# Linear attention and a gated feed-forward on one core: a new order of the steps, with trios of tiles, quartered w1 and closed first gate units

## The chip, the cores and the metric

The kernel runs on one core of a Trainium2 chip. A core has five engines that run side by side and meet through semaphores: TensorE (PE for its products and transposes, PEld for its weight loads), VectorE (DVE), ScalarE (ACT), GpSimd (POOL) and SyncE (SP), on whose queue nearly every transfer of this kernel is issued. Products land in PSUM, which DVE and ACT read and POOL does not here; operands lie in SBUF. The metric is the device time of one execution in microseconds, and lower is better.

## The reference

Eight batches of eight heads, 576 rows of 64 columns each. What is computed, in float32:

```python
def phi(x):
    return np.where(x > 0, x, np.exp(x) - 1.0) + 1.0
q_p, k_p = (phi(q), phi(k))
kv = np.einsum('bhsd,bhse->bhde', k_p, v)
z = np.sum(k_p, axis=2)
num = np.einsum('bhsd,bhde->bhse', q_p, kv)
den = np.einsum('bhsd,bhd->bhs', q_p, z)[..., None] + 1e-06
# num / den, heads side by side: x, 4608 rows of 512
a = x @ w1        # w1, w2: 512 x 1024
b = x @ w2
h = a * b @ w3    # 1024 x 1024
out = h @ w_out   # 1024 x 512
```

## The kernel before

There is no loop over the work. One string, `ORDER`, lists about 500 steps, and the kernel takes them in turn; each calls the function `s_<kind>` with its numbers. The place of a step in the list is its place on every engine's own queue that it uses: each engine takes its instructions strictly in that order and waits at the first whose inputs, or whose buffer, are not ready. A last letter names the engine that empties PSUM or casts (`a` ACT, `v` DVE, `p` POOL) or the queue of a store (`s`, `b`).

Since nothing stands between `w3` and `w_out`, their product is formed once (wf, 1024 x 512) and each token tile takes one product less. The kinds of steps are these.

- Loads, on SP: `L3.i` a 128-row tile of w3 (512 KB), `LH.0.x` half of tile 0, `LO.x` a quarter of w_out, `LA.x` and `LB.x` a quarter of w1 or w2, `LK`, `LQ`, `LV.b.h` half a batch of k, q or v (576 KB). All go into 13 buffers `ld`, so the fourteenth load waits for a buffer to be given back.
- Shapes of `LA` and `LB` (`w_part`): 0 and 1 are 256 columns of all four row blocks; 2 and 3 are two row blocks of the last 512 columns; 6 and 7 are two row blocks of the first 512 columns. Each is 1,024 values in a partition.
- `CO`, `CA`, `CB`: casts of w_out, w1, w2 to bfloat16 (1,024 columns). `C3.i` casts a w3 tile ahead of its transposes.
- `H.n.i`: n zero products of float32 that keep TensorE at work while nothing has landed; each runs as two passes in the trace.
- `T3.i.x`: four 128x128 transposes of w3 tile i, in float32 or, after `C3`, in bfloat16, and the copy out. `FW.i.x`: two of the eight 512-column products that make wf's block i; the copy out comes with x = 3.
- `EX` (exp, ACT), `PT` and `PM` (DVE) make phi of k or q. `VC` casts v. `KV.b.h` (36 products of 64x64) and `KB.b` (72, both halves) form k'v and the sums z, and cast them.
- `QP.b.h` transposes phi(q) on TensorE (nine transposes), `QD.b.h` with a DMA.
- `ND.t`: numerator and denominator of token tile t in 16 products of 64x64, with the reciprocal and the division on DVE. `NT.t`: the same for three tiles, t to t+2, in 48 products, with the reciprocals; the divisions are the separate steps `NM.t.0` to `NM.t.2`. An `ND` takes one of the two buffers `at` in PSUM, an `NT` both. `T3`, `QP` and `KV` take one too.
- `XP.t` transposes a tile of x on TensorE, `XD.c.m` two tiles with a DMA. Four tiles make a chunk c of 512 tokens.
- `F.c.f`: the gate unit f (128 columns of w1 and of w2) of chunk c: four products for a, four for b, ACT copies a out of PSUM, DVE multiplies a by b into `ab`. `FI` is one side alone. `FP` is one side on half of the chunk's tokens, in a PSUM bank that stays open until the other half; `FS` is one side on half of the tokens in a bank of its own that is emptied at once.
- `O.t`: eight products of tile t with wf, and the copy out. `S.t` stores it in two transfers. `Q.35` is the last tile in three pieces.

Two functions say the difference between the open and the closed half units:

```python
def s_FP(c0, f, side, g, e):
    f_mm(c0, f, side, slice(2 * g, 2 * g + 2))
    if g == 1:
        f_out(c0, f, side)
```

and `s_FS` takes `mm_tile(...)[:, 0:2 * P]`, runs its four products, and copies (side 0) or multiplies (side 1) its 256 columns before it gives the bank back. PSUM holds four one-bank buffers `mm` for F, FW, O, XP and KB beside the two `at`.

Lines the text speaks of: L148 zero products, L157 and L187 loads, L217, L221 and L226 the casts CO, CA and CB, L237 C3, L251 and L252 T3 and its copy, L263 and L265 FW, L273, L285 and L293 phi, L340 KV and KB, L348 and L357 their casts, L368 and L369 QP, L385 QD, L398 the products of ND and NT, L404 the divisions, L430 to L432 the reciprocals of a trio, L457 and L458 XP, L462 XD, L482 all products of F, L491 and L493 its copy and multiply, L535 and L542 O, L548 S.

Of the kernel before, what the change touches and what calls it, by code (L numbers as in the profile page):

```python
# [32 lines left out]
CA.3.a PT.q.1.0 LK.1.0 FI.0.2.1 PT.k.1.0 EX.q.1.0 PM.q.1.0 F.0.4 EX.k.1.0 PM.k.1.0 F.0.5 LV.1.0
VC.1.0.a F.0.6 LK.1.1 EX.k.1.1 PT.k.1.1 PM.k.1.1 LV.1.1 LK.3.0 KV.1.0.a VC.1.1.a F.0.7 LQ.3.1
QP.1.0.a KV.1.1.v PT.k.3.0 EX.q.3.1 EX.k.3.0 O.0.a LQ.3.0 EX.q.3.0 PT.q.3.1 ND.4 ND.5 O.1.a XP.4.a
ND.6 ND.7 PM.k.3.0 LK.2.0 XP.5.a O.2.a PM.q.3.1 XP.6.v XP.7.v LQ.2.1 EX.k.2.0 LQ.2.0 PT.k.2.0
PM.k.2.0 PT.q.3.0 EX.q.2.0 LK.3.1 PM.q.3.0 O.3.a LV.4.1 F.1.0 LV.2.0 LK.4.1 S.0.s F.1.1 PT.q.2.1
EX.q.2.1 S.1.s PT.k.3.1 F.1.2 EX.k.3.1 PM.k.3.1 LK.2.1 PM.q.2.1 F.1.3 VC.2.0.a LV.2.1 PT.k.2.1
# [6 lines left out]
XD.3.1 O.9.a O.10.a O.11.v LV.5.1 F.3.0 PM.k.5.1 LK.6.0 F.3.1 PM.k.5.0 EX.q.4.0 NM.15.1 NM.15.2
LV.5.0 S.7.s S.8.s LK.6.1 F.3.2 S.9.s S.10.s VC.5.0.v PM.q.4.0 QD.4.0 EX.k.6.0 QD.4.1 F.3.3 F.3.4
EX.q.5.1 PT.q.5.1 PM.q.5.1 PT.k.6.1 F.3.5 F.3.6 F.3.7 QD.5.1 O.12.v NT.18 QD.5.0 NM.18.0 XD.4.0
NM.18.1 VC.5.1.a PT.k.6.0 KB.5.a XD.4.1 LQ.6.1 O.13.a O.14.v PT.q.7.1 O.15.v F.4.0 EX.q.7.1 PM.q.7.1
F.4.1 F.4.2 NM.18.2 LK.7.0 F.4.3 NT.21 EX.k.6.1 NM.21.0 NM.21.1 NM.21.2 LV.6.0 VC.6.0.v F.4.4 F.4.5
S.11.s S.12.s PT.k.7.0 LK.7.1 LQ.7.0 F.4.6 LV.6.1 VC.6.1.v S.13.s S.14.s F.4.7 PT.q.7.0 PM.k.6.1  # L50
LQ.6.0 PM.k.6.0 O.16.v EX.q.7.0 O.17.v PM.q.7.0 PT.q.6.1 LV.7.0 O.18.v XD.5.0 XD.5.1 EX.q.6.1
PM.q.6.1 LV.7.1 VC.7.0.a S.15.s EX.q.6.0 KB.6.a NT.24 O.19.v NM.24.0 PT.q.6.0 PM.q.6.0 QD.6.1 F.5.0
VC.7.1.v EX.k.7.1 PT.k.7.1 F.5.1 F.5.2 EX.k.7.0 NM.24.1 NM.24.2 QD.7.1 PM.k.7.0 F.5.3 F.5.4 QD.6.0
PM.k.7.1 F.5.5 S.16.s S.17.s NT.27 XD.6.0 NM.27.0 NM.27.1 QD.7.0 KB.7.a NM.27.2 F.5.6 XD.6.1 XD.7.0
F.5.7 S.18.s NT.30 S.19.s O.20.v S.20.s F.6.0 NM.30.0 NM.30.1 NM.30.2 F.6.1 XD.7.1 O.21.v NT.33
O.22.v NM.33.0 NM.33.1 O.23.v F.6.2 F.6.3 F.6.4 F.6.5 F.6.6 F.6.7 F.7.0 F.7.1 F.7.2 F.7.3 F.7.4
# [546 lines left out]
```

## Time and profile before

| what | us |
|---|---|
| median of 3 runs (lowest, highest) | 242.84 (242.6, 242.9) |
| the profiled execution | 241.85 |
| its span, first to last instruction | 240.1 |
| PE busy | 230.6 |
| DVE busy | 158.2 |
| ACT busy | 113.9 |
| POOL busy | 1.3 |

The span is what the trace covers; the execution's own time is 1.75 us longer, for what lies around the first and the last instruction. The profile shows the busy time of each engine, the chain of work that ended last, groups of instructions with their mean durations, and what released an engine after idle time. The granted clock of TensorE was 0.997 over the span. A busy PE is not a PE at its peak, since products overlap: 512-column products start every 0.216 us in a stream, though each is shown as 0.38 us long.

### The profile page before, as it was taken

What the parts mean: (1) busy time and instruction counts of PE and PEld (TensorE: products, weight loads), DVE (VectorE), ACT (ScalarE), POOL (GpSimd) and SP (SyncE); (2) the same over time, 40 slices, a digit from 0 to 9 for tenths busy, and PEclk for the clock granted to TensorE, in tenths of its full rate; (3) what the DMA queues carried; (4) which work ended last, traced back from release to release, by engine and by line L of the source; (5) the groups of instructions that cost most, each with busy time, mean ns of one, the idle gap of its engine ahead of it and who ended that gap; (6) DMA issues with size and microseconds to landing.
All of it is one profiled execution on the core that took longest, in us unless ns stands there. A gap on an engine that the chain in (4) does not pass through costs nothing.

```text
span 240.1 us, 5470 instructions
## 1 busy us (share of the span) xinstructions
PE 230.6 (96%) x2227; PEld 115.8 (48%) x2246; DVE 158.2 (66%) x287; ACT 113.9 (47%) x166; POOL 1.3 (1%) x9
## 2 busy tenths in 40 slices
PE   7789999999999899999999999999999999999994
...
DVE  1287987989998765778865799897664343434131
...
GB/s 245 418 376 405 387 387 390 388 391 389 397 272 155 183 362 360 319 195 317 257 111 279 381 369 211 123 202 111 137 120 83 3 0 44 163 15 0 45 155 149
DMA packets 52040, 55.79 MB, mean 232 GB/s; under 512 B 31280, under 2 KB 31536, under 8 KB 52016
## 3 DMA queue, kind: packets, MB, share of 16 engines
...
## 4 chain that ended last, share of the span: by engine, by line
PE 90%; DMA 5%; DVE 1%; issue 1%; SPq 1%; ACT 0%
PE a_ps L482 26%; PE b_ps L482 26%; PE o_ps L535 24%; PE wf_ps L263 6%; DMA w<-in_moe_w_dram 3%; PE nd L398 2%; DMA qt<-phq 2%; PE w3p L251 2%; PE kbp L340 1%; PE qp L368 1%; PE xp L457 1%; PE kvp L340 1%; DVE w3t L252 1%; SPq L157 1%; DVE xt L458 0%
## 5 line engine op out<-in xcount | busy, mean ns | idle before, releaser
L482 PEld LDWEIGHTS <-w_sb 128*128 128x128 bf16 x584 | 56.4, 98 | 66.9 <-issue 0.9
L491 ACT COPY a_sb<-a_ps 128x512 f32<-128x512 f32 x72 | 42.1, 585 | 80.9 <-PE a_ps L482 79.0
L493 DVE TENSOR_TENSOR ab<-a_sb,b_ps 128x512 bf16<-128x512 f32 x72 | 49.1, 686 | 39.3 <-PE b_ps L482 37.5
L482 PE MATMUL a_ps<-xt,w_sb 128*128 128x512 bf16 (+1 forms) x296 | 74.0, 374 | 0.1
L482 PE MATMUL b_ps<-xt,w_sb 128*128 128x512 bf16 x288 | 73.8, 380 | 0.0
L535 PE MATMUL o_ps<-wf_sb,ab 128*128 128x512 bf16 (+2 forms) x290 | 63.5, 368 | 1.2 <-issue 0.6
L535 PEld LDWEIGHTS <-ab 128*128 128x128 bf16 x304 | 28.3, 98 | 31.2
L542 DVE COPY o_sb<-o_ps 128x512 f32<-128x512 f32 x23 | 15.9, 690 | 20.6 <-PE o_ps L535 19.5
L404 DVE TENSOR_TENSOR xn<-nd,r 128x512 bf16<-128x512 f32 (+2 forms) x45 | 24.3, 578 | 0.5
L273 ACT ACTIVATE eq<-q 128x1152 bf16<-128x1152 f32 x16 | 18.4, 1163 | 6.1 <-DVE phk L293 3.1
L273 ACT ACTIVATE ek<-k 128x1152 bf16<-128x1152 f32 x16 | 18.7, 1167 | 2.0 <-DMA k<-in_k_dram 1.9
L263 PE MATMUL wf_ps<-wo_sb,w3t 128*128 128x512 bf16 x59 | 15.7, 384 | 1.7 <-DVE wo_sb L217 1.0
L542 ACT COPY o_sb<-o_ps 128x512 f32<-128x512 f32 x12 | 7.0, 580 | 15.7 <-PE o_ps L535 15.7
L293 DVE TENSOR_TENSOR phq<-phq,eq 128x1152 bf16<-128x1152 bf16 x16 | 12.0, 752 | 1.4 <-ACT eq L273 0.9
L285 DVE TENSOR_SCALAR phq<-q 128x1152 bf16<-128x1152 f32 x16 | 12.1, 753 | 0.8 <-DMA q<-in_q_dram 0.8
L285 DVE TENSOR_SCALAR phk<-k 128x1152 bf16<-128x1152 f32 x16 | 12.1, 753 | 0.1
L293 DVE TENSOR_TENSOR phk<-phk,ek 128x1152 bf16<-128x1152 bf16 x16 | 12.0, 752 | 0.2
L327 ACT CAST vt<-v 128x1152 bf16<-128x1152 f32 x9 | 10.3, 1159 | 0.0
L398 PEld LDWEIGHTS <-qt 64*64 64x64 bf16 x576 | 6.3, 106 | 5.2 <-issue 3.0
L263 PEld LDWEIGHTS <-w3t 128*128 128x128 bf16 x64 | 5.6, 98 | 6.5 <-issue 1.5
L398 PE MATMUL nd<-kv,qt 64*64 64x65 bf16 x576 | 8.2, 194 | 0.5 <-DMA qt<-phq 0.5
L251 PE MATMUL w3p<-ident,w 128*128 128x128 f32 x40 | 6.9, 307 | 1.4 <-DMA w<-in_moe_w_dram 1.0
...
## 6 DMA issues: line engine op xcount, KB each, us to landing
...
```

The costliest lines, as they stand in the source:

```text
L251: nc.tensor.transpose(tp[:, c, :], blocks[:, 2 * x + c // 2, c % 2, :], idt)
L263: nc.tensor.matmul(wfs[i], w3ts[i][:, c, :], wo_sb[:, c, :], start=(c == 0), stop=(c == FC - 1))
L273: nc.scalar.activation(out=t, in_=raw[n, b, h], func=AF.Exp)
L285: (nc.gpsimd if e == "p" else nc.vector).tensor_scalar(out=by_set(n, t), in0=by_set("k", raw[n, b, h]), scalar1=0.0, scalar2=1.0, op0=ALU. ...
L293: nc.vector.tensor_tensor(out=t, in0=t, in1=by_set("k", es[n, b, h]), op=ALU.min)
L398: nc.tensor.matmul(dst[g * R:(g + 1) * R], qts[b, a // 2][rows, j, a % 2 * R:(a % 2 + 1) * R], kvs[b][rows, a // 2, a % 2, :], start=True, ...
L404: nc.vector.tensor_tensor(out=xn[:, :, a0:a1], in0=n4[:, :, :, 0:D], in1=r.unsqueeze(3).to_broadcast([P, 2, a1 - a0, D]), op=ALU.mult)
L482: nc.tensor.matmul(ops_[key][:, tiles.start * P:tiles.stop * P], w[:, w_row(kc), f * P:(f + 1) * P], xts[c0][:, tiles, kc, :], start=(kc = ...
L491: nc.scalar.copy(out=a_sbs[c0, f], in_=ops_[key])
L493: nc.vector.tensor_mul(out=abs_[c0][:, f, :], in0=a_sbs[c0, f], in1=ops_[key])
L535: nc.tensor.matmul(o_ps, abs_[c0][:, f, m * P:(m + 1) * P], wf_sb[:, f, cols], start=(f == 0), stop=(f == FC - 1))
L542: copy_of(e)(out=o_sbs[t], in_=o_ps)
```

## The change

Only the string changes; every function stays, and some that were in the file unused before are now called and others not. What the new list does:

- Tiles 0 to 2 and tiles 4 to 6 are formed by `NT.0` and `NT.4` where before `ND.0` to `ND.2` and `ND.4` to `ND.6` stood; `ND.3`, `ND.7` and `ND.8` stay single. `NT.0` stands directly behind `KV.0.1`.
- w1's first 512 columns come as `LA.0` and `LA.1` (256 columns, all rows) for `LA.6` and `LA.7`; w2's stay row halves.
- The first four units of chunk 0 are 16 `FS` steps for four `FP` and six `FI`.
- Eight zero products for five.
- Six weight casts go to POOL: `CO.2`, `CA.0`, `CA.2`, `CA.3`, `CB.6` and `CB.7`.
- Of the 35 `O` steps 22 are emptied by ACT and 13 by DVE, for 12 and 23.
- The whole list is in another order: w3's tile 7 comes first and three w3 tiles come ahead of w_out, `NT.15` and `KB.4` stand apart, `O.4` stands ahead of `NT.9`, `O.28` to `O.31` stand among the units of chunk 8.

The diff, its first part and the places named:

```diff
-I.0 H.3.0 L3.2 LO.0 I.1 T3.2.0.a H.1.1 CO.0.v FW.2.0.a T3.2.1.a H.1.2 LO.1 CO.1.a L3.4 T3.4.0.v
-T3.4.1.v L3.3 T3.3.0.a LO.2 FW.4.0.v FW.4.1.a LO.3 L3.5 T3.3.1.v C3.5.a CO.2.v FW.2.1.a FW.2.2.a
-CO.3.v FW.2.3.v L3.6 C3.6.v FW.3.0.a FW.3.1.v LK.0.0 T3.5.0.v LH.0.0 T3.5.1.v LQ.0.0 FW.4.2.v
...
-FW.7.2.a KV.0.0.a PM.k.0.1 VC.0.1.v FW.7.3.v FW.1.3.a KV.0.1.v T3.0.1.a ND.0 FW.0.0.v LA.6 ND.1
-FW.0.1.v CA.6.a LA.7 CA.7.a ND.2 FW.0.2.a XP.0.a XP.1.a ND.3 FW.0.3.a FP.0.0.0.0 LB.6 LQ.1.1
-EX.q.1.1 LB.7 LA.3 XP.2.v XP.3.v FP.0.1.0.0 CB.7.a LA.2 FP.0.1.0.1 LB.3 PT.q.1.1 PM.q.1.1 FI.0.2.0
...
-EX.k.4.1 KB.2.a QD.2.0 VC.3.1.a ND.8 QD.3.0 F.1.7 KB.3.a NT.9 NM.9.0 NM.9.1 QD.3.1 XD.2.0 NM.9.2
-XD.2.1 S.2.s LK.4.0 O.4.v O.5.v NT.12 LV.4.0 NM.12.0 O.6.v NM.12.1 O.7.v NM.12.2 LQ.4.1 PT.k.4.0
...
+L3.7 L3.4 L3.2 LO.1 I.0 H.1.1 H.3.0 H.1.2 I.1 T3.4.0.a H.2.3 T3.2.0.v T3.2.1.a T3.4.1.v H.1.4 C3.7.a
+T3.7.0.v LO.0 CO.0.a LO.2 CO.1.v FW.2.0.a T3.7.1.a LO.3 FW.4.0.a CO.3.a LQ.0.0 L3.6 FW.7.0.a
+PT.q.0.0 L3.1 FW.2.1.a FW.4.1.a EX.q.0.0 LQ.0.1 PM.q.0.0 CO.2.p FW.2.2.a FW.7.1.a FW.7.2.v FW.7.3.a
+FW.4.2.a FW.4.3.v QP.0.0.v C3.6.a LK.0.0 T3.1.0.a T3.1.1.a PT.q.0.1 FW.2.3.v L3.3 L3.5 T3.6.0.v
+T3.6.1.v EX.q.0.1 LK.0.1 FW.1.0.a FW.1.1.a PT.k.0.0 FW.1.2.a PM.q.0.1 FW.6.0.a FW.6.1.v FW.6.2.v
...
+LH.0.1 FW.3.0.a FW.3.1.v T3.5.1.a FW.3.2.v FW.3.3.v PM.k.0.1 LA.0 LB.6 I.2 CA.0.p CB.6.p LB.7
+PM.k.0.0 T3.0.0.a LA.1 FW.5.0.a VC.0.0.a QP.0.1.v FW.0.0.a FW.0.1.a KV.0.0.a LA.2 VC.0.1.v FW.5.1.v
+T3.0.1.v KV.0.1.a NT.0 NM.0.0 NM.0.1 CB.7.p FW.0.2.a FW.0.3.a NM.0.2 FW.5.2.a FW.5.3.a LA.3 XP.0.a
+CA.2.p XP.1.v ND.3 LB.2 CA.1.v XP.2.a LB.3 FS.0.0.0.0 FS.0.1.0.0 FS.0.1.1.0 FS.0.0.1.0 LQ.1.1 LK.1.0
+XP.3.v FS.0.2.0.0 FS.0.2.1.0 FS.0.2.0.1 FS.0.2.1.1 CB.2.v FS.0.0.0.1 FS.0.0.1.1 FS.0.1.0.1
+FS.0.1.1.1 FS.0.3.0.1 CB.3.v PT.q.1.1 CA.3.p F.0.4 EX.q.1.1 PM.q.1.1 PT.k.1.0 LQ.1.0 LV.1.0 PT.q.1.0
...
+LV.2.0 FS.0.3.1.1 EX.q.3.1 NT.4 NM.4.0 NM.4.1 O.1.a NM.4.2 EX.q.2.1 PT.q.2.1 LK.2.0 XP.4.a ND.7
...
+PM.k.3.0 QD.3.1 F.1.6 F.1.7 O.4.a PM.q.3.0 PT.q.5.1 QD.3.0 NT.9 KB.3.a O.5.a NM.9.0 O.6.a NM.9.1
+NM.9.2 NT.12 NM.12.0 NM.12.1 NM.12.2 O.7.a XD.2.0 XD.2.1 LV.4.0 F.2.0 LQ.4.0 EX.q.5.1 F.2.1 NT.15
...
+S.26.s S.27.s F.7.7 F.8.0 F.8.1 F.8.2 O.28.v O.29.v S.28.s O.30.a O.31.v F.8.3 S.29.s S.30.s S.31.s
+F.8.4 F.8.5 F.8.6 F.8.7 O.32.v O.33.v S.32.s O.34.a S.33.s S.34.b Q.35
```

More of the change, by code (lines that the diff above doesn't have):

```diff
@@ L21 @@
 ORDER = """
-I.0 H.3.0 L3.2 LO.0 I.1 T3.2.0.a H.1.1 CO.0.v FW.2.0.a T3.2.1.a H.1.2 LO.1 CO.1.a L3.4 T3.4.0.v
-T3.4.1.v L3.3 T3.3.0.a LO.2 FW.4.0.v FW.4.1.a LO.3 L3.5 T3.3.1.v C3.5.a CO.2.v FW.2.1.a FW.2.2.a
-CO.3.v FW.2.3.v L3.6 C3.6.v FW.3.0.a FW.3.1.v LK.0.0 T3.5.0.v LH.0.0 T3.5.1.v LQ.0.0 FW.4.2.v
-EX.k.0.0 PT.k.0.0 FW.4.3.a EX.q.0.0 T3.6.0.v PM.k.0.0 FW.5.0.v FW.5.1.v L3.1 T3.6.1.a PT.q.0.0
-PM.q.0.0 L3.7 FW.5.2.v FW.6.0.a FW.3.2.a FW.3.3.v FW.5.3.v LQ.0.1 T3.1.0.a C3.7.v T3.1.1.a FW.1.0.v
@@ L33 @@
[L33 to L38, printed above, removed]
@@ L45 @@
[L45 to L50, printed above, removed]
@@ L51 @@
[L51 to L56, printed above, removed]
@@ new lines @@
+FW.4.2.a FW.4.3.v QP.0.0.v C3.6.a LK.0.0 T3.1.0.a T3.1.1.a PT.q.0.1 FW.2.3.v L3.3 L3.5 T3.6.0.v
+T3.6.1.v EX.q.0.1 LK.0.1 FW.1.0.a FW.1.1.a PT.k.0.0 FW.1.2.a PM.q.0.1 FW.6.0.a FW.6.1.v FW.6.2.v
+LH.0.0 EX.k.0.0 T3.3.0.a T3.3.1.a FW.1.3.a C3.5.v T3.5.0.a FW.6.3.v EX.k.0.1 PT.k.0.1 LV.0.0 LV.0.1
+LH.0.1 FW.3.0.a FW.3.1.v T3.5.1.a FW.3.2.v FW.3.3.v PM.k.0.1 LA.0 LB.6 I.2 CA.0.p CB.6.p LB.7
+PM.k.0.0 T3.0.0.a LA.1 FW.5.0.a VC.0.0.a QP.0.1.v FW.0.0.a FW.0.1.a KV.0.0.a LA.2 VC.0.1.v FW.5.1.v
+T3.0.1.v KV.0.1.a NT.0 NM.0.0 NM.0.1 CB.7.p FW.0.2.a FW.0.3.a NM.0.2 FW.5.2.a FW.5.3.a LA.3 XP.0.a
@@ new lines @@
+CA.2.p XP.1.v ND.3 LB.2 CA.1.v XP.2.a LB.3 FS.0.0.0.0 FS.0.1.0.0 FS.0.1.1.0 FS.0.0.1.0 LQ.1.1 LK.1.0
+XP.3.v FS.0.2.0.0 FS.0.2.1.0 FS.0.2.0.1 FS.0.2.1.1 CB.2.v FS.0.0.0.1 FS.0.0.1.1 FS.0.1.0.1
+FS.0.1.1.1 FS.0.3.0.1 CB.3.v PT.q.1.1 CA.3.p F.0.4 EX.q.1.1 PM.q.1.1 PT.k.1.0 LQ.1.0 LV.1.0 PT.q.1.0
+EX.k.1.0 FS.0.3.0.0 LK.1.1 F.0.5 F.0.6 PM.k.1.0 VC.1.0.v EX.q.1.0 PM.q.1.0 QP.1.1.a EX.k.1.1
+FS.0.3.1.0 PT.k.1.1 LV.1.1 F.0.7 KV.1.0.a LQ.2.1 LQ.3.1 VC.1.1.a QP.1.0.a O.0.a PM.k.1.1 KV.1.1.v
+LV.2.0 FS.0.3.1.1 EX.q.3.1 NT.4 NM.4.0 NM.4.1 O.1.a NM.4.2 EX.q.2.1 PT.q.2.1 LK.2.0 XP.4.a ND.7
```

30 lines of the change are left out of this document (20 added, 10 removed).

## The prediction

> **What bounds the kernel now.** I read the page first (busy slices, then the chain that ended last), then busy time by stage, then TensorE's own timeline with the releaser of each gap.
>
> ```profile
> PE   7789999999999899999999999999999999999994
> DVE  1287987989998765778865799897664343434131
> PE 90%; DMA 5%; DVE 1%; issue 1%; SPq 1%; ACT 0%
> ```
>
> ```profile
> 6.00:14.00 8.00, 5.77 (x33) 3.96 (x33) 2.93 (x6) 2.35 (x4) 0.00 (x0) 1.00 1.02 415
> 14.00:34.00 20.00, 19.14 (x253) 11.29 (x257) 16.62 (x32) 13.92 (x20) 0.00 (x0) 1.00 1.04 388
> 34.00:60.00 26.00, 25.65 (x282) 13.73 (x283) 22.87 (x46) 22.90 (x31) 0.00 (x0) 1.00 1.05 389
> 60.00:84.00 24.00, 23.32 (x350) 11.61 (x352) 21.35 (x40) 13.80 (x21) 0.00 (x0) 1.00 1.02 252
> 84.00:234.50 150.50, 149.77 (x1280) 70.30 (x1288) 92.56 (x163) 58.51 (x90) 0.00 (x0) 1.00 0.66 175
> 234.50:240.10 5.60, 2.17 (x26) 1.76 (x24) 0.97 (x3) 0.58 (x1) 0.00 (x0) 0.87 0.57 143
> ```
>
> The columns of the second fence are the stretch, its length, then busy time of PE, PEld, DVE, ACT and POOL, the granted clock, the DMA share and GB/s. TensorE is the bound. From 14 us on it is busy 96 to 99% of every stage, so a new order can win only where TensorE still waits: 2.2 us of idle between 6 and 14, and some tenths in each later stage. DVE and ACT run at 88% from 34 to 60 us, and the DMA engines are full until 60, so a step put too early waits for one of these. The 5.6 us after the last full products are the same pieces, copies and stores in both orders.
>
> ```profile
> 1.18 2.93 PE L148 MATMUL warm<-zero 128*128 128x256 f32 x6 [1.18 <-DVE zero L135]
> 8.76 1.21 PE L251 MATMUL w3p<-ident,w 128*128 128x128 f32 x8 [0.97 <-DMA w<-in_moe_w_dram]
> 13.74 1.84 PE L263 MATMUL wf_ps<-wo_sb,w3t 128*128 128x512 bf16 x7 [0.95 <-DVE wo_sb L217]
> 17.17 1.03 PE L263 MATMUL wf_ps<-wo_sb,w3t 128*128 128x512 bf16 x4
> 34.37 0.60 PE L482 MATMUL a_ps<-xt,w_sb 128*128 128x256 bf16 x4
> 5.34 0.69 DVE L217 CAST wo_sb<-wo 128x1024 bf16<-128x1024 f32 x1 [4.22 <-DMA wo<-in_moe_w_out_dram]
> 13.76 1.05 ACT L237 CAST w3b<-w 128x1024 bf16<-128x1024 f32 x1 [2.12 <-DMA w<-in_moe_w_dram]
> 19.12 0.76 DVE L285 TENSOR_SCALAR phq<-q 128x1152 bf16<-128x1152 f32 x1 [0.52 <-DMA q<-in_q_dram]
> ```
>
> TensorE's rows, then three first uses. The uses date the loads: the second lands by 5.34, the eighth by 13.76, the twelfth by 19.12, so 1.3 to 1.4 us each, one after another. Whatever stands n-th in the new list lands at about the time of the n-th of the old one.
>
> **The change, part by part.** Units first.
>
> ```profile
> 8.73 1.04 PEld L251 LDWEIGHTS w3p<-ident,w 128*128 128x128 f32 x8 [1.34 <-issue]
> 17.11 0.23 PE w3p L251 x4
> 18.42 2.16 PE wf_ps L263 x10
> 20.76 0.53 issue
> 26.44 1.17 PE L368 MATMUL qp<-ident,phq 128*128 128x128 bf16 x18
> 27.27 0.75 DVE L369 COPY qt<-qp 128x1152 bf16<-128x1152 bf16 x1
> ```
>
> A T3 step of float32 takes 0.5 us of TensorE, of bfloat16 0.23; one 512-column product 0.216, so an FW step 0.43; a QP step 0.58.
>
> *Start to 17.2 us.* The new list loads three w3 tiles before any w_out. The third lands near 7.3 (the fourth at 8.76 by its row). T3.2.0 and T3.2.1 then end at 8.4, and ACT has in a row T3.2.1's cast (0.58), C3.7 (1.05) and CO.0 (1.05, fifth load, landed by 9.9): 8.6 + 0.6 + 1.0 + 1.0 = 11.2 for the first FW, which before starts at 6. From 11.2 the new order has work enough: 6.0 us of it by 17.2, on top of four float32 and one bfloat16 T3 (2.2), 8.2 in all. Before, at 17.17, ten FW, six float32 and three bfloat16 T3 are done: 4.3 + 3.0 + 0.7 = 8.0. Even, so 0; bounds -0.5 to +0.7.
>
> *Three more zero products* (8 for 5): two passes each of 0.43 to 0.49 by the first row. They stand in front of data not yet landed, but two of them (H.2.3) run from about 6.3 to between 7.2 and 8.0 where T3.2.0 could start at 7.3: 0 to +0.7, I take +0.1.
>
> *17.2 us to the first gate product.* Work left before: 4 float32 and 3 bfloat16 T3, 22 FW, 2 QP, two KV, four ND and two XP.
>
> ```profile
> 98.80 0.82 PE kbp L340 x70
> 161.61 0.51 PE nd L398 x47
> 162.12 0.65 PE kbp L340 x68
> 163.74 0.86 PE b_ps L482 x4
> 166.33 0.51 PE nd L398 x48
> 168.68 0.86 PE a_ps L482 x4
> ```
>
> A visit to 64x64 products, net of the eight or four full products before the next row: 168.68 - 166.33 - 8 x 0.216 = 0.62 us for 48, and 163.74 - 161.61 - 0.86 = 1.27 for 120. So 9 ns a product and 0.18 us a visit, whatever it holds. Tiles 0 to 2 in one trio and KV.0.1 before it make six visits three: -0.54. New waits in this stretch, followed through the list: T3.1.1 needs the bank that QP.0.0's copy (0.75) frees, 0.6, where before T3.1.1 waits as long (the row of 20.76 above is this wait); T3.6.1 waits 0.2; NT.0 stands right behind KV.0.1 and needs its cast kv, which T3.0.1 covered before.
>
> ```profile
> 28.66 0.27 ACT L348 CAST kv<-kvp 128x130 bf16<-128x130 f32 x1
> 76.06 0.17 DVE L430 TENSOR_SCALAR r<-nd 128x14 f32<-128x14 f32 x1 [0.34 <-PE nd L398]
> 76.80 1.95 DVE L404 TENSOR_TENSOR xn<-nd,r 128x512 bf16<-128x512 f32 x4
> ```
>
> That wait is 0.13 + 0.27 + 0.1 = 0.5. Behind NT.0, DVE needs 0.74 + 1.95 = 2.7 us (second and third row) and XP.1's copy 0.33 before the first FS, 3.1 in all with latency; TensorE has four FW, three XP and ND.3 to put beside it, 2.6: 0.5 to 0.9 open. New waits 1.8 to 2.2 in sum against 1.0 before (34.2 - 17.2 = 17.0 less work of about 16.0, the visits among it). With the visits: 2.0 - 1.0 - 0.54 = +0.5 at the first gate product, range -0.3 to +1.3.
>
> *Closed units and quarters.* 16 FS steps of 256 columns are 64 products for 24 of 512 and 16 of 256: 64 x 0.108 = 6.9 either way. The two quarters of w1 let units 0 and 1 begin on one load; they wait for xt, not for w1, so 0.
>
> *POOL casts.* Six casts of 1,024 columns leave ACT and DVE for POOL.
>
> ```profile
> L138 POOL CAST ident<-ident 128x128 bf16<-128x128 f32 x1 | 0.3, 289 | 0.1
> L226 DVE CAST w_sb<-wb 128x1024 bf16<-128x1024 f32 x3 | 2.1, 687 | 0.0
> ```
>
> No row shows one. Bounds: 0.69 us (DVE's) and 8 x 0.289 = 2.3; taking 0.1 as fixed, 0.1 + 8 x 0.19 = 1.6. At 1.6, CO.2 (sixth load, 11.2) ends at 12.8, used at 13.7; CA.0, CB.6 and CB.7 (loads 20 to 22, from 30) end at 34.9, used at 35.8; CA.2 and CA.3 at 37.2 and 38.8, used at 41. Hidden; at 2.3 the third delays by 1.3 at most. [...] Beside them stand DVE's casts CO.1 (11.1) and CA.1 (36), each on the path within 0.7 us. What a POOL cast does to a DVE cast no row shows: 0 to 2.3 us. I take 0.4, half a cast that is met once in two.
>
> *F.0 to F.2.0.* Four visits before and after, then three and three. ND.7 waits for a bank that NM.4.1 frees: +0.3; NT.4 for KV.1.1's cast: +0.1. DVE is freer: 13 O evacuations for 23, at 0.7 us each, the others on ACT; TensorE's gaps there are not DVE's, so 0. One wait goes:
>
> ```profile
> 79.66 0.41 PE L398 MATMUL nd<-kv,qt 64*64 64x65 bf16 x25
> 80.53 0.38 PE L398 MATMUL nd<-kv,qt 64*64 64x65 bf16 x23 [0.47 <-DMA qt<-phq]
> 81.08 3.40 PE L535 MATMUL o_ps<-wf_sb,ab 128*128 128x512 bf16 x15 [0.16 <-issue]
> 173.78 0.58 PE L398 MATMUL nd<-kv,qt 64*64 64x65 bf16 x48
> 174.52 3.40 PE L535 MATMUL o_ps<-wf_sb,ab 128*128 128x512 bf16 x15 [0.16 <-issue]
> xt<-xn SPq DMA_TRANSPOSE x14, 3.3
> ```
>
> NT.12 costs 81.08 - 79.66 = 1.42, the undisturbed NT.33 0.74: 0.68 for a late transpose of q. The new order puts O.4 ahead of NT.9 and O.5, O.6 ahead of NT.12, 3.5 us: -0.68. Next late is XD.2.1, which SP can issue only when NM.9.2 is done; 3.3 us to land brings it to within some tenths of F.2.0: 0 to +0.6, I take 0.
>
> *F.2.0 to the end.* Eight visits for seven (NT.15 and KB.4 apart): +0.18; the 0.17 that KB.4 took longer than KB.7 (0.82 at 98.80 against 0.65) goes. O.28 to O.31 move in among F.8; O.32 behind F.8.7 needs its last unit 1.5 us after it starts, and DVE delivers it in 0.9: 0.
>
> Sum: 0 + 0.1 + 0.5 + 0.4 + 0.4 - 0.68 + 0.18 - 0.17 = +0.7, with the half-open XD.2.1 +0.8. The profiled execution is 241.85 us (span 240.1); the median of the runs is 242.84, 1.0 above. Predicted profile 242.7, runs 243.6.
>
> **The rivals.** *Faster:* NT.0's front is not late. If the first gate product starts by 34.5 (XP.2, 0.25 of work, now lies ahead of it), the 0.5 becomes 0, the 0.4 of F.0 goes with it, and 242.84 - 0.68 + 0.18 - 0.17 = 242.2; if the start also gains what three visits less are worth (0.54), 241.6; I put 241.9. For it: DVE is freer and two casts leave ACT's way at the start. Against: NT.0's chain through DVE is longer than the work beside it.
> *POOL holds DVE off:* CO.1 behind CO.2 delays FW.2.1 by 0.7, CA.1 behind CA.2 and CA.3 delays FS.0.2.0.0 by 0.8 to 1.6; both decide once POOL starts first: +1.5 to +2.3 less the 0.4 taken, 245.2. [...]
> *No change:* the late front and the gone wait cancel, and no cast is met: 242.84 + 0.1 + 0.5 + 0.4 - 0.68 = 243.2.
>
> **How the numbers follow.** A measurement can tell 0.2% here (0.5 us). Forecast 0.42 (243.3 to 244.6), POOL 0.18, no change 0.15, faster 0.25. So faster 0.25, same 0.15, slower 0.60. The range leaves a tenth on either side: 241.7 to 245.4.
>
> **What would show it.** First FW near 11.2; a gap of 0.5 before NT.0; first gate product near 35.0; POOL casts near 1.6 us, and DVE casts of 0.69 stretched or late beside them; NT.12 at 0.62. The prediction is wrong if the start loses or gains a microsecond, which only the landing of the first five loads decides, or if a later stage shows a gap that I found covered.

## The result, and the profile after

The changed kernel takes 241.56 us (median of 10 runs, 240.87 to 242.02), the kernel before beside it 242.75 (10 runs, 242.12 to 243.9): a ratio of 0.9943, 95% interval 0.9919 to 0.9968. It is faster by about half a percent, where 243.6 and slower was forecast. The profiled execution of the changed kernel took 241.54 us (span 239.7), that of before 241.85 (240.1). So there are two things to explain: 0.4 us between the two spans, and some 0.8 more between the medians.

The page of the changed kernel, in its parts on busy time, slices and the chain:

```profile
PE 233.2 (97%) x2276; PEld 120.2 (50%) x2276; DVE 151.0 (63%) x278; ACT 115.0 (48%) x173; POOL 8.1 (3%) x15
...
PE   8899999999999999999999999999999999999994
...
DVE  0347787889999646877862588885546363433341
...
PE 96%; DVE 1%; ACT 1%; issue 0%
```

TensorE is the bound as before, with a chain of 96% for 90%; the DMA entry of before (5%) has gone from it. DVE has 7 us less to do, POOL 7 us more. TensorE's timeline of the changed kernel (start, length, operation, count, idle before and its releaser), the rows at the places that the prediction named. Line numbers are one higher than before (L483 gate unit, L516 closed half unit, L399 nd, L264 wf):

```profile
11.67 0.59 PE L264 MATMUL wf_ps<-wo_sb,w3t 128*128 128x512 bf16 x2 [0.54 <-ACT wo_sb L218]
...
18.25 0.74 PE L252 MATMUL w3p<-ident,w 128*128 128x128 f32 x4 [0.37 <-DVE qt L370]
...
31.15 0.58 PE L399 MATMUL nd<-kv,qt 64*64 64x65 bf16 x48 [0.37 <-DVE w3t L253]
31.66 1.90 PE L264 MATMUL wf_ps<-wo_sb,w3t 128*128 128x512 bf16 x8
33.40 0.71 PE L458 MATMUL xp<-ident,xn 128*128 128x128 bf16 x8
...
34.78 1.03 PE L516 MATMUL a_ps<-xt,w_sb 128*128 128x256 bf16 x8
...
59.77 1.03 PE L483 MATMUL a_ps<-xt,w_sb 128*128 128x512 bf16 x4
...
81.20 0.58 PE L399 MATMUL nd<-kv,qt 64*64 64x65 bf16 x48
81.71 1.90 PE L536 MATMUL o_ps<-wf_sb,ab 128*128 128x512 bf16 x8
83.45 1.03 PE L483 MATMUL a_ps<-xt,w_sb 128*128 128x512 bf16 x4
```

After 31.15 no row of PE has a wait of 0.3 us. NT.12 (81.20) takes 0.51 to the next step, where before it took 1.42. The table has the start of the first product of four steps, in us, for the two kernels and the experiments below; the last columns are the lengths of the stretches between them.

| trace | first gate product | F.1.0 | F.2.0 | Q.35 | gate to F.1.0 | F.1.0 to F.2.0 | F.2.0 to Q.35 |
|---|---|---|---|---|---|---|---|
| before | 34.37 | 59.99 | 84.31 | 234.74 | 25.62 | 24.32 | 150.43 |
| b_copy | 34.62 | 60.24 | 84.62 | 235.81 | 25.62 | 24.38 | 151.19 |
| b_nt12 | 34.69 | 60.31 | 83.99 | 234.24 | 25.62 | 23.68 | 150.25 |
| b_h8 | 35.04 | 60.65 | 85.12 | 236.59 | 25.62 | 24.47 | 151.47 |
| b_both | 35.73 | 61.36 | 85.60 | 236.01 | 25.62 | 24.24 | 150.41 |
| b_split | 36.36 | 61.98 | 86.43 | 237.00 | 25.62 | 24.45 | 150.57 |
| after | 34.78 | 59.77 | 83.45 | 234.21 | 24.99 | 23.68 | 150.77 |
| a_copy | 35.04 | 60.03 | 83.70 | 234.35 | 24.99 | 23.67 | 150.65 |
| a_nd0 | 34.99 | 59.98 | 83.67 | 234.29 | 24.98 | 23.70 | 150.62 |
| a_nd4 | 34.15 | 59.52 | 83.18 | 233.79 | 25.37 | 23.66 | 150.62 |
| a_open | 34.58 | 61.02 | 84.68 | 235.49 | 26.43 | 23.67 | 150.81 |
| a_rows | 34.54 | 60.98 | 84.66 | 235.43 | 26.44 | 23.68 | 150.77 |
| a_moved | 34.39 | 59.73 | 83.39 | 234.17 | 25.34 | 23.67 | 150.78 |
| a_best | 34.40 | 59.38 | 83.06 | 233.69 | 24.98 | 23.68 | 150.63 |

Against before's own profile the changed kernel is 0.41 late at the first gate product, wins 0.63 from there to F.1.0 and 0.64 to F.2.0, and gives back 0.34 to Q.35 and 0.12 behind it: 0.41 - 0.63 - 0.64 + 0.34 + 0.12 = -0.4, the difference of the spans. The stretches repeat from trace to trace within 0.15 us or so, but for the 150.43 of before, to which the last group of experiments comes; the first gate product does not repeat.

Of the 0.63 between the first gate product and F.1.0, some 0.22 are XP.2 (four transposes of 0.056), which now lies ahead of that product. The rest are two waits of before, in the rows of its weight loads, with the idle time ahead of each:

```profile
35.22 0.23 PEld L457 LDWEIGHTS <-xn 128*128 128x128 bf16 x4 [0.20 <-DVE xn L404]
...
36.14 1.83 PEld L482 LDWEIGHTS <-w_sb 128*128 128x128 bf16 x11 [0.25 <-issue]
```

XP.3 waits 0.20 for the division of tile 3, and the half unit behind it, which needs the transposed tile 3, waits 0.25. PE's own rows show neither: a busy row covers each (34.80 to 35.62, 35.46 to 38.46).

### The profile page after: what moved, and what is told of

Its sections match the earlier page's. It is cut to its first block, busy times and chain, and to the rows that moved or that the text cites. A ratio compares the mean times of both kernels' runs of the same rounds, so it can differ in the third digit from the quotient of the medians.

```text
span 239.7 us, 5540 instructions
## 1 busy us (share of the span) xinstructions
PE 233.2 (97%) x2276; PEld 120.2 (50%) x2276; DVE 151.0 (63%) x278; ACT 115.0 (48%) x173; POOL 8.1 (3%) x15
## 4 chain that ended last, share of the span: by engine, by line
PE 96%; DVE 1%; ACT 1%; issue 0%
PE o_ps L536 26%; PE a_ps L483 25%; PE b_ps L483 24%; PE wf_ps L264 6%; PE nd L399 3%; PE w3p L252 3%; PE warm L149 2%; PE kbp L341 2%; PE a_ps L516 2%; PE b_ps L516 2%; PE xp L458 1%; PE qp L369 1%; PE kvp L341 1%; ACT wo_sb L218 0%; ACT w3b L238 0%; DVE w3t L253 0%
## 5 line engine op out<-in xcount | busy, mean ns | idle before, releaser
L483 PEld LDWEIGHTS <-w_sb 128*128 128x128 bf16 x544 | 52.6, 98 | 62.5 <-DVE xt L459 0.3
L494 DVE TENSOR_TENSOR ab<-a_sb,b_ps 128x512 bf16<-128x512 f32 x68 | 46.2, 686 | 39.9 <-PE b_ps L483 38.6
L492 ACT COPY a_sb<-a_ps 128x512 f32<-128x512 f32 x68 | 39.8, 586 | 64.0 <-PE a_ps L483 63.6
L483 PE MATMUL a_ps<-xt,w_sb 128*128 128x512 bf16 x272 | 69.9, 380 | 0.0
L483 PE MATMUL b_ps<-xt,w_sb 128*128 128x512 bf16 x272 | 69.8, 379 | 0.0
L536 PE MATMUL o_ps<-wf_sb,ab 128*128 128x512 bf16 (+2 forms) x304 | 65.2, 368 | 0.0
L543 ACT COPY o_sb<-o_ps 128x512 f32<-128x512 f32 x22 | 12.9, 586 | 33.5 <-PE o_ps L536 26.7
L543 DVE COPY o_sb<-o_ps 128x512 f32<-128x512 f32 x13 | 9.0, 691 | 15.3 <-PE o_ps L536 12.6
L264 PE MATMUL wf_ps<-wo_sb,w3t 128*128 128x512 bf16 x64 | 15.6, 380 | 0.5 <-ACT wo_sb L218 0.5
L264 PEld LDWEIGHTS <-w3t 128*128 128x128 bf16 x64 | 5.9, 98 | 5.8 <-issue 0.7
L328 ACT CAST vt<-v 128x1152 bf16<-128x1152 f32 x7 | 8.1, 1162 | 0.9 <-DMA v<-in_v_dram 0.9
L253 ACT CAST w3t<-w3p 128x512 bf16<-128x512 f32 x7 | 4.0, 587 | 9.3 <-PE w3p L252 7.4
L399 PEld LDWEIGHTS <-qt 64*64 64x64 bf16 x576 | 6.1, 106 | 4.3 <-issue 4.1
L399 PE MATMUL nd<-kv,qt 64*64 64x65 bf16 x576 | 7.6, 194 | 0.4 <-DVE w3t L253 0.4
```

The costliest lines, as they stand in the source:

```text
L264: nc.tensor.matmul(wfs[i], w3ts[i][:, c, :], wo_sb[:, c, :], start=(c == 0), stop=(c == FC - 1))
L399: nc.tensor.matmul(dst[g * R:(g + 1) * R], qts[b, a // 2][rows, j, a % 2 * R:(a % 2 + 1) * R], kvs[b][rows, a // 2, a % 2, :], start=True, ...
L483: nc.tensor.matmul(ops_[key][:, tiles.start * P:tiles.stop * P], w[:, w_row(kc), f * P:(f + 1) * P], xts[c0][:, tiles, kc, :], start=(kc = ...
L492: nc.scalar.copy(out=a_sbs[c0, f], in_=ops_[key])
L494: nc.vector.tensor_mul(out=abs_[c0][:, f, :], in0=a_sbs[c0, f], in1=ops_[key])
L536: nc.tensor.matmul(o_ps, abs_[c0][:, f, m * P:(m + 1) * P], wf_sb[:, f, cols], start=(f == 0), stop=(f == FC - 1))
```

## The experiments

Line numbers in the experiments' rows are one to three below those of the kernel they are made from. Edits are shown as the steps taken out of and put into the list.

**Parts of the first gate units.** One run makes units 0 and 1 open again and units 2 and 3 whole, the next gives w1's first half back in row halves.

```
a_open   - FS.0.0.* FS.0.1.* FS.0.2.* FS.0.3.*
         + FP.0.0.*.* FP.0.1.*.* (open, both sides), FI.0.2.0 FI.0.2.1 FI.0.3.0 FI.0.3.1 (whole)
a_rows   - LA.0 LA.1 CA.0.p CA.1.v
         + LA.6 LA.7 CA.6.p CA.7.v
```

> The changed kernel with the first three units open instead of closed: units 0 and 1 as four FP pairs in four banks that wait for XP.3's copy, units 2 and 3 whole. Theory G (closed units gained, because other work can be put where an open unit waits for tiles 2 and 3): TensorE waits 0.7 to 1.3 us between XP.3 and the second halves, F.0.4 comes at 41.3 to 41.9 for 40.57 and F.1.0 keeps it; ratio 0.997 to 1.000. Theory P (POOL's casts and the order gained): less than 0.3 us at F.1.0, ratio as the changed kernel (0.994).

> The changed kernel with w1's first half as two row halves (LA.6, LA.7) for the two column quarters, cast at the same places. The first gate product then needs both loads: the second lands at 34.6 and its cast on DVE stands behind ND.3, done at 36.3, where the first gate product of the changed kernel is at 34.75. Theory Q (the quarters let the units begin on one load): the first gate product at 36.3 to 36.5, +1.6 us, kept at F.1.0; ratio 1.000 to 1.001. My prediction's claim (the units wait for xt, not for w1): less than 0.3 us.

a_open: 242.73 us, ratio to before 1.0023 [1.0001, 1.0044]; a_rows: 243.2, 1.0037 [1.0011, 1.0063]. Either one takes the whole gain away. TensorE's timeline of a_open, then of a_rows:

```profile
36.79 0.60 PE L481 MATMUL b_ps<-xt,w_sb 128*128 128x256 bf16 x4 [0.52 <-DVE xt L457]
...
42.32 0.82 PE L481 MATMUL b_ps<-xt,w_sb 128*128 128x512 bf16 x3 [0.38 <-DVE w_sb L225]
...
54.12 0.52 PE L397 MATMUL nd<-kv,qt 64*64 64x65 bf16 x39 [0.32 <-DVE kv L347]
```

```profile
34.54 0.27 PE L514 MATMUL a_ps<-xt,w_sb 128*128 128x256 bf16 x1
36.09 0.94 PE L514 MATMUL a_ps<-xt,w_sb 128*128 128x256 bf16 x7 [1.28 <-DVE w_sb L220]
```

With open units TensorE waits for the transposed tile 3, then for a cast of w2, and NT.4 waits for the cast of k'v, since no half unit stands ahead of it any more; with row halves it stands 1.3 us in the second product for the cast of the second half of w1's rows. Both make gate to F.1.0 1.45 longer. The new order needs both parts; the old order, with open units and row halves, had 0.45 us of waits there; its units stood in another sequence. So 1.45 is what leaving out either part costs at these places of this order, and 0.4 what the stretch won.

**GpSimd's casts.** First the six casts go back to ACT and DVE at the places where they stood in the list, then at places where their loads have landed.

```
a_nopool  CO.2.p CB.6.p CB.7.p -> .v, CA.0.p CA.2.p CA.3.p -> .a, same places
a_moved   CO.2.v behind LO.3; CA.0.a CB.6.a behind NT.0; CB.7.v behind XP.1;
          CA.2.a behind FS.0.0.1.0; CA.3.a behind FS.0.2.1.1
```

> The changed kernel with the six POOL casts back on ACT (CA.0, CA.2, CA.3) and DVE (CO.2, CB.6, CB.7), nothing else moved. If the first gate units gained because POOL took the casts: the waits of about 0.8 us return between 34 and 42 us, and XP.1's copy comes 0.6 to 1.2 us later on DVE (CB.7 stands ahead of NM.0.2), so the first gate product comes at 35.4 to 36 for 34.75; ratio to before 0.998 to 1.001. If they gained because of the closed units and the order: at most 0.3 us of loss.

> The changed kernel with its six GpSimd casts given back to DVE and ACT, each at a place of that engine's list where its load has landed by the changed kernel's trace (CO.2 on DVE behind the fourth w_out load, CA.0 and CB.6 on ACT behind NT.0, CB.7 on DVE behind XP.1, CA.2 and CA.3 on ACT among the first gate units). Theory 1, the worth of GpSimd is the engine time that it takes off ACT and DVE: the first gate product 0.3 to 0.8 us later, F.1.0 0.3 to 1.0 later, 242.0 to 242.5. Theory 2, the worth was only that no load is waited for in the two in-order lists: within 0.3 us of the changed kernel (241.6), 6 us below the run that gave the casts back at their old places (247.5). Theory 3, GpSimd casts hold DVE off as the prediction's rival had it: faster than the changed kernel by 0.4 or more.

a_nopool: 247.53 us, 1.0231 [1.0198, 1.0263], far above the 0.998 to 1.001 expected; a_moved: 241.39, 0.9931 [0.9906, 0.9956], no slower than the changed kernel. Its gate to F.1.0 is 0.35 longer (0.25 of it a wait for a cast of w1 on DVE), but its first gate product stood 0.39 earlier. So the 6 us of the first (247.53 for 241.39) are not what the casts cost: they are what an in-order queue costs that holds a cast ahead of its load. TensorE's timeline of a_nopool:

```profile
12.00 1.67 PE L262 MATMUL wf_ps<-wo_sb,w3t 128*128 128x512 bf16 x7
16.66 2.75 PE L262 MATMUL wf_ps<-wo_sb,w3t 128*128 128x512 bf16 x12 [2.99 <-DVE wo_sb L216]
```

The casts themselves, in the timelines of POOL and of DVE in the changed kernel:

```profile
11.72 1.37 POOL L218 CAST wo_sb<-wo 128x1024 bf16<-128x1024 f32 x1 [10.07 <-DMA wo<-in_moe_w_out_dram]
...
30.44 1.04 POOL L222 CAST w_sb<-wa 128x1024 bf16<-128x1024 f32 x1 [16.99 <-DMA wa<-in_moe_w_dram]
...
35.99 1.18 POOL L222 CAST w_sb<-wa 128x1024 bf16<-128x1024 f32 x1 [1.78 <-DMA wa<-in_moe_w_dram]
```

```profile
11.51 0.68 DVE L218 CAST wo_sb<-wo 128x1024 bf16<-128x1024 f32 x1
...
35.59 0.68 DVE L222 CAST w_sb<-wa 128x1024 bf16<-128x1024 f32 x1
```

A cast takes 1.04 us on POOL. In this trace DVE came first at both places, ran its 0.68 unstretched, and POOL paid: 0.33 for an overlap of 0.47, 0.14 for one of 0.28. In a_h5, a run that comes below, POOL came first at both places. Its POOL, its DVE and the weight loads of TensorE:

```profile
11.38 1.04 POOL L216 CAST wo_sb<-wo 128x1024 bf16<-128x1024 f32 x1 [9.72 <-DMA wo<-in_moe_w_out_dram]
...
36.12 1.04 POOL L220 CAST w_sb<-wa 128x1024 bf16<-128x1024 f32 x1 [1.79 <-DMA wa<-in_moe_w_dram]
```

```profile
12.23 1.09 DVE L216 CAST wo_sb<-wo 128x1024 bf16<-128x1024 f32 x1
...
36.42 1.29 DVE L220 CAST w_sb<-wa 128x1024 bf16<-128x1024 f32 x1
```

```profile
37.77 1.75 PEld L514 LDWEIGHTS <-w_sb 128*128 128x128 bf16 x16 [0.20 <-DVE w_sb L220]
```

There POOL ran its 1.04, and DVE's casts took 1.09 and 1.29. The second lost 0.61 for an overlap of 0.74, and TensorE waited 0.20 for it. The first lost 0.41 for an overlap of 0.19 with the cast of POOL, which was busy for 0.36 us more with two further instructions between that cast and 14 us. So in none of the four pairs was the first one stretched, and in three of them the second lost the overlap less some 0.14 us (0.33 of 0.47, 0.14 of 0.28, 0.61 of 0.74). Why it loses that much no run shows. The 1.6 that the prediction took for a POOL cast stands against these 1.04.

**Trios.**

```
a_nd0   - NT.0 NM.0.0 NM.0.1 .. NM.0.2     + ND.0 .. ND.1 .. ND.2, between the FW behind it
a_nd4   - NT.4 NM.4.0 NM.4.1 .. NM.4.2     + ND.4 ND.5 .. ND.6 (ahead of ND.7)
```

> The changed kernel with the trio of tiles 0 to 2 taken apart: ND.0, ND.1 and ND.2 between the FW steps that stand behind it, as before. The prediction's step: two visits more at 0.18 us (+0.36) against a shorter chain through DVE ahead of the first FS (-0.3 to -0.5): first gate product -0.2 to +0.1 us, 241.4 to 241.7. Rival, the chain through DVE is hidden by the work beside it and the visits count in full: +0.3 to +0.5, 242.0.

> The changed kernel with tiles 4, 5 and 6 as three ND in the places that they have before (4 and 5 ahead of O.1, 6 with 7). Products and visits are as many; ND costs DVE 0.4 us more. By the price of a visit (0.18 us): 0 to +0.2 us at F.1.0, ratio 0.994 to 0.996. If the trio is what the order lives on: over 0.5 us.

a_nd0: 242.25 us, 0.9965 [0.9941, 0.9988], where a_moved and a_start beside it on the same chip have 0.9931 and 0.9938. From KV.0.1 (30.09) to the first gate product (34.99) it needs 4.90 us, the changed kernel 34.78 - 30.30 = 4.48. The trio is worth 0.42: two visits at 0.18 and nothing lost to a longer chain through DVE. The rows of the changed kernel say why: from 31.66 to 34.78 TensorE has work without a gap, 3.1 us of it. a_nd4: 241.44, 0.9963 [0.9949, 0.9977]; its gate to F.1.0 is 0.38 longer where at most 0.2 was expected, since XP.7 waits 0.31 for the division of tile 7. The times do not show it (241.44 for 241.56), the ratios could (0.9963 for 0.9943). That trio is worth some 0.4 us in the profile; what it is worth in the runs is not settled.

**NT.12's wait.** The kernel before with one step moved.

```
b_nt12   O.4.v O.5.v + O.6.v NT.12 LV.4.0 NM.12.0 - O.6.v NM.12.1
```

> The kernel before with one step moved: O.6 ahead of NT.12, so that 15 full products more (with O.4 and O.5) stand in front of the tiles that wait for a transposed q. The prediction's step: NT.12 falls from 1.42 us to 0.6 to 0.75, F.2.0 starts 0.5 to 0.7 us earlier against F.1.0, and all of it reaches the end: about 242.1. Rival: what is next late at that place (the transposes of x for tile 2, issued behind NM.9 and NM.12) takes the gain back, F.2.0 not earlier by more than 0.2 us, 242.7.

242.23 us, 0.9982 [0.9953, 1.001]. Its timeline:

```profile
81.74 0.58 PE L396 MATMUL nd<-kv,qt 64*64 64x65 bf16 x48
82.25 1.90 PE L533 MATMUL o_ps<-wf_sb,ab 128*128 128x512 bf16 x8
```

NT.12 is down to 0.51 and F.1.0 to F.2.0 by 0.64 against before, all of which is still there at Q.35. The runs agree in size but their interval does not exclude nothing.

**Start of the changed kernel.**

```
a_h5     - H.1.1 - H.2.3
a_start  LO.0 ahead of LO.1; C3.7.a -> C3.7.v, early; T3.7.0, T3.7.1 and CO.0 earlier; FW.2.3 between T3.1.0 and T3.1.1
a_best   a_start, and T3.0.1 KV.0.1 ahead of FW.5.1 (NT.0 then has FW.5.1 ahead of it)
a_copy   no edit
```

> The changed kernel with five zero products for eight: H.1.1 and H.2.3 are left out. Theory A: it loses 0.3 to 0.9 us against the changed kernel (ratio to before 0.996 to 0.998). Theory B: no loss; the first T3 comes up to 0.3 us earlier and the ratio stays near 0.994 to 0.995.

> The changed kernel with its start ordered differently: C3.7 on DVE, which is idle there, instead of ACT; LO.0 ahead of LO.1; CO.0 ahead of T3.2.1's copy; both T3.7 earlier; FW.2.3 between the two T3.1. Theory that the late first FW (11.67 us) and T3.1.1's wait cost time: first FW at 10.3 to 10.8, the first gate product 0.3 to 1.0 us earlier, 240.6 to 241.3. Rival, the loads one after another set the first gate product whatever the order ahead of them: first FW earlier, the first gate product within 0.2 us, 241.6.

> The changed kernel with the other start (as in the run of the start) and with T3.0.1 and KV.0.1 ahead of FW.5.1, so that the casts that NT.0 waits for have FW.5.1's two products beside them. Theory, NT.0's wait of 0.37 us is on the path: first gate product 0.3 to 0.5 us earlier than the changed kernel's 34.75, 241.0 to 241.2. Rival, the chain of tile 0 through DVE ahead of the first unit sets it: first gate product within 0.2 us, 241.3 to 241.5.

> The changed kernel as it is, a second profiled execution of it. Theory, the changed kernel's executions are alike where before's are not: steps within 0.1 us of the first profile from the first gate product on, no gap where before has its gap at 150 us, all runs within 241.0 to 242.2. Rival, it has the same kinds of executions as before, only fewer of the long ones: a run above 242.8, or a step from the first gate product on that differs by 0.5 us or more from the first profile.

a_h5: 242.46 us, 0.9995 [0.997, 1.0019]. Two runs of twelve took 240.5, the others 241.8 to 243.2: without these two steps it can be faster, but mostly isn't. Its profiled execution took 242.44. TensorE's timeline of a_h5 and of the changed kernel:

```profile
10.37 1.06 PE L147 MATMUL warm<-zero 128*128 128x256 f32 x2
```

```profile
9.99 0.60 PE L149 MATMUL warm<-zero 128*128 128x256 f32 x2
```

The same zero product takes 1.06 us for 0.60. By the granted clock's records the clock is full from 12.98 us in the one and from 7.13 in the other, so at 10 us it is full in the second alone; how low it was in a_h5 no record shows, and 0.60 / 1.06 puts it near half, an estimate. The first gate product is 0.83 later (35.61), and from there to F.1.0 it takes 25.29, 0.30 more, with the wait of 0.20 behind DVE's stretched cast that was shown above. a_start: 241.29, 0.9938 [0.9916, 0.996]: the first FW begins 1.1 earlier (10.56), the first gate product 0.17. So the first FW does not set it: TensorE then waits 0.78 for phi(q), whose first step on DVE had waited 2.47 for the load of q (2.29 in the changed kernel). a_best: 241.23, 0.9928 [0.9898, 0.9957]; a_copy beside it 241.34, 0.9918 [0.9891, 0.9945]. NT.0's wait is gone and the first gate product is at 34.40, and still the runs cannot tell the two apart. TensorE's timeline of a_best:

```profile
30.22 0.61 PE L262 MATMUL wf_ps<-wo_sb,w3t 128*128 128x512 bf16 x2
30.76 0.58 PE L397 MATMUL nd<-kv,qt 64*64 64x65 bf16 x48
```

a_copy missed what was expected at the start (0.26 later than the first profile; one run, 240.53, below the band given) and met the rest: from the first gate product to Q.35 it takes 199.30 us against 199.43, and its longest run of six is 241.57.

**Why before's median lies a microsecond above its profile.**

```
b_copy   no edit
b_h8     H.1.2 -> H.3.2, + H.1.5 ahead of FW.2.2
b_split  NT.24 behind O.19
b_both   b_h8 and b_split together
```

> The kernel before once more, unchanged, for a second profile of it. The two profiles on record differ by 0.3 us (241.85 and 241.54) where the medians of ten runs differ by 1.2, so 0.9 us lies in what varies from execution to execution of the kernel before. Theory A (the start: the moment at which TensorE's clock is granted in full, against products that are waiting): this profile is 0.3 to 1.5 us longer than 241.85, and the difference stands before 14 us. Theory B (the transfers: the late transpose of q at NT.12 and the loads): the difference stands at 79 to 81 us or in loads that land late. Ratio to the kernel before 1.000 within its interval.

> The kernel before with three more zero products, two behind H.1.2 and one ahead of FW.2.2, where TensorE waits anyway. Theory A: TensorE is kept at work, the full clock comes as early as in the changed kernel in every run, and the runs fall by 0.3 to 0.9 us, with a narrower spread. Theory B and the theory that only the gate units and NT.12 count: no change, within 0.2%.

> The kernel before with NT.24 behind O.19 instead of directly behind KB.6, so that no 120 small products stand in a row there. The second profile of the kernel before has TensorE still for 0.7 to 1.1 us at 150 us, in the middle of O.19, waiting for nothing that the profile shows, and a 16 KB transfer of the instruction queue at 148.5 us; the first profile has that transfer at 146 us and no gap. Theory C (TensorE is out of instructions after 120 small products, 240 instructions in 1.3 us): no gap at 150, one visit more (+0.18), the runs fall by 0.4 to 0.8 us to a ratio of 0.997 to 0.998. Rival (the gap is a slow transfer that can come at any place): the gap stays or moves, ratio 1.000 to 1.002.

> The kernel before with both repairs of its start and its gap at 150 us, neither of which moved the median alone: the three zero products of the changed kernel (H.3.2 for H.1.2, H.1.5 ahead of FW.2.2), and NT.24 behind O.19. Theory, before's median lies a microsecond above its profiled execution because each execution meets either a clock that falls back at the start or the gap at 150 us: with both repaired no gap at 150 us, the granted clock full from 6 us on, a median of 241.7 to 242.1 and no execution above 242.8. Rival, what makes before's other executions longer is neither of the two: median 242.5 to 242.8, with executions above 243.2 as before.

b_copy: 242.51 us, 0.9988 [0.9968, 1.0008]; b_h8: 242.56, 0.9999 [0.998, 1.0019]; b_split: 242.85, 1.0019 [0.9995, 1.0042]; b_both: 242.65, 0.9976 [0.9953, 0.9999], which misses the 241.7 to 242.1 of its theory. b_split was expected at 0.997 to 0.998 and missed it too. The profile of b_copy is 1.1 us longer than before's, 0.25 of it ahead of the first gate product and 0.76 behind F.2.0. The profiles of the four show three things that come and go.

The first is a gap at 150 us, absent in before and b_nt12, there in b_copy and b_h8 with the same order at that place. The timelines of b_copy, then of b_h8:

```profile
149.56 0.82 PE L533 MATMUL o_ps<-wf_sb,ab 128*128 128x512 bf16 x2
151.08 1.24 PE L533 MATMUL o_ps<-wf_sb,ab 128*128 128x512 bf16 x5 [0.71 <-issue]
```

```profile
149.43 0.60 PE L396 MATMUL nd<-kv,qt 64*64 64x65 bf16 x45
151.06 0.22 PE L396 MATMUL nd<-kv,qt 64*64 64x65 bf16 x3 [1.03 <-issue]
```

F.4.0 to F.5.0 takes 22.60 us without it, 23.54 and 23.83 with it. It waits for nothing that the profile shows. A 16 KB transfer on the queue named "instruction" starts at 146.0 and 145.6 in the two traces without a gap and at 148.5 and 148.4 in the two with it, so late code for the 120 small products of KB.6 and NT.24 is the reading at hand, argued and not shown. With NT.24 behind O.19 there is no gap (b_split, b_both), though in b_split that transfer starts at 150.3, about as late behind its F.4.0 as in b_copy (19.7 us for 19.9).

The second is the clock. b_split by windows (stretch, length, busy time of PE, PEld, DVE, ACT, POOL, granted clock, DMA share, GB/s):

```profile
4.41:7.82 3.41, 2.58 (x14) 1.73 (x14) 0.69 (x1) 1.16 (x2) 0.00 (x0) 1.00 0.94 374
7.82:11.23 3.41, 1.35 (x9) 1.19 (x10) 0.90 (x2) 1.06 (x2) 0.00 (x0) 1.00 1.03 419
11.23:14.65 3.42, 3.42 (x13) 2.28 (x14) 0.39 (x1) 0.66 (x2) 0.00 (x0) 0.50 1.02 406
14.65:18.06 3.41, 2.46 (x12) 0.94 (x11) 2.58 (x5) 1.72 (x2) 0.00 (x0) 1.00 1.01 347
```

After a stretch in which TensorE was busy 1.35 of 3.41 us, waiting for w3, the clock is at half for 3.42 us, with TensorE busy all of it, and about 1.7 us of work are lost, an estimate from half of 3.42. What makes it fall, and what sets the length, no run shows. The changed kernel is busy 1.70 of the 2 us from 8 to 10, where before is busy 1.21 and b_split 0.43.

How often the clock falls can be read from the mean granted clock that is on record for every execution: 3.42 us at half make it 0.993, as in b_split's profile. Of 113 executions of the kernel before that were timed beside the runs of this section (one of 345.65 us left out), 13 have 0.993 or less, and in each of the four groups these are on average 0.8 to 1.2 us longer than the others. None of the 24 of b_h8 and b_both has it, and none of the 16 of the changed kernel. So the zero products go with a clock that does not fall, but a fall in one execution of nine is worth some 0.1 us in the mean: it is not what lifts before's median. (The late clock of a_h5 does not show in this figure: its profile, with the clock full from 12.98 us, has 1.0.)

The third is the loads. The timelines of TensorE in b_copy, then in b_both, and of DVE in b_both:

```profile
8.46 1.20 PE L249 MATMUL w3p<-ident,w 128*128 128x128 f32 x8 [0.79 <-DMA w<-in_moe_w_dram]
```

```profile
9.54 1.20 PE L249 MATMUL w3p<-ident,w 128*128 128x128 f32 x8 [1.02 <-DMA w<-in_moe_w_dram]
...
29.44 0.48 PE L338 MATMUL kvp<-vt,phk 64*64 64x65 bf16 x36 [0.95 <-DVE qt L367]
```

```profile
27.96 0.77 DVE L325 CAST vt<-v 128x1152 bf16<-128x1152 f32 x1 [1.02 <-DMA v<-in_v_dram]
```

The second tile of w3 sets the same step at 8.46, 8.76 (before) and 9.54, and v can hold up DVE, and TensorE's KV.0.0 behind it, by a microsecond that before's first profile does not have. So before's first gate product lies between 34.37 and 36.36, and the profile that the prediction was made from is the earliest of six; their mean is 35.14, and 35.01 without b_h8 and b_both, whose front has three more zero products. The changed kernel's, in the five traces with all eight zero products, the POOL casts and the trio in front of it (after, a_copy, a_open, a_rows, a_nd4), lies between 34.15 and 35.04, mean 34.62.

That makes a balance between ordinary executions rather than between two profiles: front -0.5, gate to F.1.0 -0.6, F.1.0 to F.2.0 -0.7, F.2.0 to Q.35 +0.3, behind it +0.1, and the gap at 150 us (mean of 22.60, 22.60, 23.54 and 23.83, less 22.60) -0.5: -1.9, or -1.4 without the gap. The two comparisons of the changed kernel gave 0.9943 and 0.9918, 1.4 and 2.0 us, with intervals of 0.8 to 2.0 and 1.3 to 2.6. Both sums fit, so the balance does not tell whether the gap counts. It comes from few profiles, and on before's side from uneven ones: b_copy, b_h8 and b_split were profiled in the longest execution of their runs, and before itself in one that is shorter than all of the ten beside the result. What stays open is why each repair alone, and both together, moved before's median so little: b_both has neither gap nor a falling clock, in its profile the front came 1.4 us later than before's, and its median is 242.65.

## Why the prediction was wrong

The time is the one of the rival named *Faster*, 241.56 for its 241.9, but its condition, a first gate product by 34.5, was not met in either profile of the changed kernel (34.78 and 35.04); that its figure is close is in part luck. The forecast was 2.0 us too high: 1.2 in the profile (242.7 for 241.54), 0.9 in what was laid on top for the runs.

- *From profile to runs.* "The median of the runs is 242.84, 1.0 above" was carried over to the changed kernel whole. That microsecond belongs to executions of the order before, whose front comes up to 2 us later than in the profile that was read; how much of it each cause makes stays open. The changed kernel's profile lies 0.02 from its median. This step failed, and with it 0.9 of the 2.0 us.
- *Closed units and quarters, 0.* This step failed. "They wait for xt, not for w1": in a_rows TensorE waits 1.28 us for the cast of w1. Without either part the new order is 1.45 longer here, and against before it won 0.41 by waits that are gone, XP.2 apart.
- *F.0, +0.4.* This step failed: ND.7's and NT.4's waits did not come, the changed kernel has neither. With the 0.25 of XP.2 this stretch had been priced at -0.25 + 0.4 = +0.15, and it measured -0.63: 0.8 of the 1.2 us in the profile.
- *POOL casts, +0.4.* Hidden, as the terms had it, but 1.04 us long and not 1.6, and in the changed kernel's profiles DVE was not held, since DVE came first wherever two casts met. The mechanism of the rival on POOL is there all the same: in a_h5 POOL came first at both places and DVE's second cast took 0.61 longer. Its price was too high: TensorE waited 0.20 for it, where 0.8 to 1.6 had been put at that place.
- *Start and 17.2 us to the first gate product, +0.6, or +0.85 with XP.2.* Measured +0.41 against before's profile, 34.78 and 35.04 for "near 35.0", NT.0's wait 0.37 for 0.5 (its row names T3.0.1's copy on DVE, which ends when the cast of k'v does), first FW 11.67 for 11.2. The place was right, and the comparison not: against the mean of 35.0 to 35.1 of before's profiles nothing was lost. The waits before were taken as 1.0 from a first gate product at 34.2, which the row has at 34.37. The 0.5 to 0.9 open behind NT.0 were a mis-sized term: the work beside the chain is 3.1 us, not 2.6. The trio's gain of visits came in full (a_nd0, 0.42).
- *Zero products, +0.1.* Their cost was right in before's order (b_h8: no change), their use was missed. In the changed kernel, two of the steps taken out move the median by +0.9; the profile of that run shows the clock full only from 12.98 us. Five of its twelve runs have a mean granted clock of 0.991 to 0.993; whether the clock accounts for every long run of a_h5 is open.
- *NT.12, -0.68.* Right: -0.64 alone in before's order, -0.64 in the change. XD.2.1 was not late.
- *F.2.0 to the end, 0.* +0.34 to Q.35 and +0.12 behind it, 0.45 more than priced. No run took it apart. By the products' starts the visit more costs its 0.2, and the 0.17 taken off for KB.4 did not stay: from its first product to its last KB.4 fell from 0.79 to 0.59, but KB.6 and KB.7 rose from 0.59 and 0.62 to 0.73 and 0.69. What lies behind Q.35 varies from 5.3 to 6.0 in the traces of the changed kernel and its variants.
